# Windowed attention with sinks, then a squared-ReLU MLP, on one core: batch 0's last third loaded before w_out, its second 256 tokens masked by VectorE, scores of the first 256 tokens first

## The chip, the cores and the metric

One core of a Trainium2 chip. The time is device microseconds of one execution. The kernel before took 226.03 us (median of 8 runs, 225.04 to 226.9).

## What is computed

For each of 4 batches and 8 heads (768 tokens, head size 64): attention in which token *t* sees the 128 tokens that end with itself, and the first 4 tokens (the sinks). The heads' outputs side by side are the rows `x` of an MLP with a squared ReLU.

```python
scores = scale * np.matmul(q, k.transpose(0, 1, 3, 2))
keep = is_sink | in_window          # pos < 4, or 0 <= t - pos < 128
scores = np.where(keep, scores, -1000000000.0)
a = np.exp(scores - np.max(scores, axis=-1, keepdims=True))
a = a / (np.sum(a, axis=-1, keepdims=True) + 1e-09)
x = np.matmul(a, v)                 # to (B * S, H * D) = (3072, 512)
r = np.maximum(x @ w_in, 0.0)       # w_in 512 x 2048
return (r * r) @ w_out              # w_out 2048 x 512
```

## The kernel before, in words

**Work per batch.** A batch's 768 tokens are three steps `s` of 256; its 8 heads are four pairs `m`. For batches 0 and 1, q and k arrive as f32 in `qr` (line 348), are cast and regrouped into `qs` (helper lines 206, 208, 210 by engine), turned by TensorE into the PSUM tile `pt` (476), and copied into `qkT` by two copies for each `pt`. They are loaded in two groups, the first 512 tokens (group 0) and the last 256 (group 1). For batches 2 and 3 the loads cast (`qn`, 380) and the DMA turns (436).

Then, for each step and pair: scores into `ps` (571), exp on ScalarE into `expm` (590), a mask, and values times `expm` into `po` (634), with the sinks of tokens beyond 256 from a tile `pk` of their own (531, exp 539). Row sums come with `po`: VectorE takes reciprocals (645) and scales into `xn_sb` (646). `px` (671) turns it, a copy puts it in `xT`. Layer 1 is `pm` (694), its ReLU on ScalarE (703), its square on VectorE into `gT` (710); layer 2 is `py` (734), copied to `osb` and stored (750). Below, `b0 s1` is batch 0's step 1.

**Two ways to mask.** In general the mask is a multiplication of `expm` by the tile `mask` (`mask0` for step 0, whose sinks lie inside) on VectorE (599), or a selection on GpSimd (222). In batch 0 with `s < BIASED = 2` there is none: two matmuls of `bias` with the identity (564) put -30000 into `ps` before the scores. The mask tiles are built by GpSimd late (`build_masks`, 252 to 257), from `tri`.

**Order.** Nothing is scheduled on the chip. While the program is built, `Plan.run` (58) takes at each step, among the operations whose predecessors are planned, the one with the earliest planned start, then the lowest key, and puts it on the engine that would end it first. `PE_SLACK`, a DMA's `margin`, the costs in the braces and the keys (`at(...)`, `LO`, `HI`) act on that order alone. Each engine then executes its list in order. PSUM has four tiles, two in the pool `att`, two in `den`; `pm` and `py` take `den` tiles.

**Loads.** SP issues the `qr` loads; GpSimd issues `v` (361, called v0 to v5 for batch 0's six tiles), `w_in` (300, quarters 0 to 3) and `w_out` (307, quarters 0 to 3). `behind` makes an issue wait until another load has landed. Before: SP's group 1 of batch 0 waits for w_out 0; GpSimd issues w_in 0 to 3, w_out 0 and 1, then waits for group 1's second k load, issues w_out 2, v4, v5, w_out 3; SP's loads of batch 1 wait for v5.

```python
    load_w_out(0, None, ())
    load_w_out(1, None, ())
    for m0 in (0, 2):
        for ti in (1, 0):
            load_qk(0, m0, ti, 1, 2, ("w_out", 0) if m0 == 0 and ti == 1 else None, [("w_out", 1)])
    load_w_out(2, ("qk", 0, 2, 1, 1), [("qk", 0, 2, 0, 1)])
    load_v(0, 2, None, ())
    load_w_out(3, None, ())
```

TensorE's list begins with turns and 72 filler matmuls (201) that work on the identity while data is awaited; then all of b0 s0 and s1 up to `px`; then 128 `pm` (four blocks of 16 for each step); then `py` of steps 0 and 1 (64), mixed with step 2 and batch 1.

Of the kernel before, what the change touches and what calls it, by code (L numbers as in the profile page):

```python
# [16 lines left out]
LATENCY = 0.2  # L17
PE_SLACK = 0.334
DMA_START = {"sp": 1.2, "act": 1.2, "pool": 1.6}
# [114 lines left out]
def kernel(  # L134
# [11 lines left out]
    nc = tc.nc  # L146
# [11 lines left out]
    NSINK = 4  # L158
# [92 lines left out]

    def build_masks(e):
        for h2 in range(2):
            for i in range(2):
                nc.gpsimd.tensor_copy(out=mask[:, h2, 2 * i:2 * i + 2, :], in_=tri)
                nc.gpsimd.tensor_copy(out=mask0[:, h2, 2 * i:2 * i + 2, :], in_=tri)
            nc.gpsimd.memset(mask0[0:NSINK, h2, 1:3, :], 1.0)

# [10 lines left out]
    c_ident = op(-9, {"pool": 0.3}, build_ident)  # L269
    c_tri = op(-0.15, {"pool": 0.6}, build_triangles)  # L270
    c_bias = op(-8, {"pool": 1.3}, build_bias)
    c_sinks = op(-7, {"pool": 0.5}, build_head_rows)


# [93 lines left out]
    def load_natural(b, s, older_values):  # L368

        begun = [ops["layer1", b - 2, 0, 0], w_out_op[3]]  # L370
        for ti in (1, 0):
            if s == 0:
                qn_slot[b, ti] = Slot("qr", NT)
            for i in range(2):
                t = 2 * s + i

                def run(e, t=t, ti=ti):
                    if t == 0:
                        qn_t[b, ti] = work["qr"].tile([128, NT, DM], BF16, name="qn", tag="qr")
                    return [nc.gpsimd.dma_start(  # L380
                        out=qn_t[b, ti][:, t, :].rearrange("p (h d) -> p h d", d=D),
                        in_=(q, k)[ti][b, :, 128 * t:128 * t + 128, :].rearrange("h p d -> p h d"))]
                o = dma_op("pool", ("qk", b, ti, t), run, 64 * 0.032,
                           None,
                           [qn_slot[b, ti]] if t == 0 else ())
                o.after += begun
                o.margin = 1.661
        for t in (2 * s, 2 * s + 1):
            def run(e, t=t):
                return [nc.gpsimd.dma_start(  # L390
                    out=v_sb[b % 2][:, t, :, 0:D],
                    in_=v[b, :, 128 * t:128 * t + 128, :].rearrange("h p d -> p h d"))]
            o = dma_op("pool", ("v", b, t), run, 64 * 0.032)
            o.after += begun + older_values
            o.margin = 1.661

# [5 lines left out]
    def attention(b, key):  # L402
# [16 lines left out]
        def stage(g, f0, f1, side):  # L419
# [9 lines left out]
            if b in NATURAL:  # L429
                for s in range(NS):  # L430
                    for ti in (1, 0):
                        for i in range(2):
                            t = 2 * s + i

                            def turn(e, s=s, ti=ti, i=i, t=t):
                                nc.sync.dma_start_transpose(
                                    out=qkT_sb[:, :, ti, t, :], in_=qn_t[b, ti][:, t, :])
                            ops["turn", b, ti, t] = op(
                                at(0.1 * s), {"sp": 1.25}, turn, dma=0.3, reads=[qn_slot[b, ti]],
                                after=[ops["qk", b, ti, t]] + prev_scores + prev_sinks)  # L440
                            ops["turn", b, ti, t].margin = 5.167
                            copies.append(ops["turn", b, ti, t])
                    ops["cast", b, s] = ops["v", b, 2 * s + 1]
# [101 lines left out]
            for s in range(t0 // 256, last // 256):  # L545
# [3 lines left out]
                for m0 in (0, 2):  # L549
# [26 lines left out]
                    sc = []  # L576
                    for ms in ((m0,), (m0 + 1,)) if b == 0 else ((m0, m0 + 1),):
                        sc.append(op(
# [3 lines left out]
                                   for t in range(max(0, 2 * s - 1), 2 * s + 2)] if b in NATURAL else  # L582
                            [c for m in ms for gg in range(g + 1) for c in ops["copies", b, m, gg]]))
                        ops["scores", b, s, ms[0]] = sc[-1]
                    masked = []
                    o = 0 if s else 128
                    for j, m in enumerate((m0, m0 + 1)):
# [19 lines left out]
                        if biased:  # L607
                            masked.append(ex)
                            continue
                        first = b == 0 and s < 2  # L610
                        masked.append(op(at(fm + 0.03), {"pool": 1.3} if first else
                                         {"pool": 1.3, "dve": 0.7} if s else {"dve": 0.58, "pool": 1.1},
                                         domask, after=[ex] if first else [ex, late["masks"]]))

# [39 lines left out]
                if b in NATURAL or b == 1 and s in TURNED:  # L654
                    for t in (2 * s, 2 * s + 1):
                        def turn_x(e, t=t):
# [3 lines left out]
                                ([o_] if t % 2 else []))  # L660
                        o_.margin = 2.284
                    ops["bridge", b, s] = ops["xT", b, s] = o_
# [113 lines left out]

    NATURAL, TURNED, BIASED = (2, 3), (), 2
    load_sinks("act", 0)
# [7 lines left out]
    for i in range(4):  # L786
        load_w_in(i, None if i == 0 else None)
    load_w_out(0, None, ())
    load_w_out(1, None, ())
    for m0 in (0, 2):  # L790
        for ti in (1, 0):
            load_qk(0, m0, ti, 1, 2, ("w_out", 0) if m0 == 0 and ti == 1 else None, [("w_out", 1)])
    load_w_out(2, ("qk", 0, 2, 1, 1), [("qk", 0, 2, 0, 1)])
    load_v(0, 2, None, ())
    load_w_out(3, None, ())
    for m0 in (0, 2):
        for ti in (1, 0):
            load_qk(1, m0, ti, 0, 2, ("v", 0, 5) if m0 == 0 and ti == 1 else None, [("w_out", 3)])
    for m0 in (0, 2):
# [5 lines left out]

    LO, HI = 0.12, 0.624
    for b in range(B):
        if b == 0:
            at = attention(0, lambda f: f - 1.0)
            at(0, 0.0, 1.0, ("den", "att"))  # L810
            late["masks"] = op(0.006, {"pool": 3.0}, build_masks, after=[c_tri, ops["bridge", 0, 1]])
            at(1, 0.2, 0.725, "att")
        if b == 0:
# [3 lines left out]
        else:  # L817
            for i, fb in enumerate(range(0, NFB, 2)):
                layer1(b, b + 0.34 * i / 8, (fb, fb + 1), 0, 512, (0, 1))
        for i, fb in enumerate(range(0, NFB, 4)):  # L820
            if b == 0:
                layer1(b, 0.2 + 0.226 * i / 4, range(fb, fb + 4), 512, 256, (2,))
            else:
                layer1(b, b + 0.34 + 0.167 * i / 4, range(fb, fb + 4), 512, 256, (2,))
        if b + 1 < B:
# [3 lines left out]
            if b == 0:  # L829
                at = attention(1, lambda f: f)  # L830
                at(0, 0.179, 0.751, ("att", "den"))
                at(1, 0.369, 0.369, ("att", "den"))
            else:
                attention(b + 1, lambda f, b=b: b + LO + (HI - LO) * f)(0, 0.0, 1.0, "att")
        for u in range(NS):
            if b == 0 and u < 2:
                layer2(b, u, lambda i, part, u=u: 0.408 + 0.466 * (4 * part + 2 * u + i) / 24, by_part=True)
            else:
# [37 lines left out]
```

The softmax here doesn't subtract the row's maximum and nothing guards it: scores larger than these inputs give would overflow.

## Time and profile before

| | |
|---|---|
| median of 8 runs | 226.03 us |
| the profiled execution | 225.62 us, of it the span 223.9 us |
| mean granted TensorE clock | 1.000 |
| TensorE (PE) busy | 216.9 us, 97% of the span |
| VectorE (DVE), ScalarE (ACT), GpSimd (POOL) busy | 104.0, 115.9, 65.1 us |
| `py`, line 734 | 384 matmuls, 88.5 us |
| `pm`, line 694 | 576 matmuls, 86.7 us |
| HBM read, written | 27.30 MB, 6.29 MB |
| chain that ended last, by line | pm 38%, py 38%, po 6%, ps 5% |

All times are counted from the first instruction of the span. In a timeline, the first number is the start, the second the length; a bracket tells how long the engine was idle before and what ended that. The chain is the work that ended last, followed back from the end. A matmul's own duration (379 ns for 512 columns) contains its passage through the array; back to back they are issued faster (1.73 us for 8 of them in the chain).

### The profile page before, as it was taken

What the parts mean: (1) busy time and instruction counts of PE and PEld (TensorE: products, weight loads), DVE (VectorE), ACT (ScalarE), POOL (GpSimd) and SP (SyncE); (2) the same over time, 40 slices, a digit from 0 to 9 for tenths busy, and PEclk for the clock granted to TensorE, in tenths of its full rate; (3) what the DMA queues carried; (4) which work ended last, traced back from release to release, by engine and by line L of the source; (5) the groups of instructions that cost most, each with busy time, mean ns of one, the idle gap of its engine ahead of it and who ended that gap; (6) DMA issues with size and microseconds to landing.
All of it is one profiled execution on the core that took longest, in us unless ns stands there. A gap on an engine that the chain in (4) does not pass through costs nothing.

```text
span 223.9 us, 4606 instructions
## 1 busy us (share of the span) xinstructions
PE 216.9 (97%) x1952; PEld 138.0 (62%) x1952; DVE 104.0 (46%) x192; ACT 115.9 (52%) x131; POOL 65.1 (29%) x99
## 2 busy tenths in 40 slices
PE   7899999999999999999999999999999999999993
PEld 7549996467865896555454545598464455874441
DVE  6656356466756764466462536657241024430010
ACT  2695556506893577286727188665351165551010
POOL 7991015046999335996300000000000000000000
PEclk9999999999999999999999999999999999999999
DMA  6999976998999999999999463020221320000222
GB/s 179 258 161 208 214 212 101 225 327 244 129 179 136 141 201 140 106 155 204 145 141 150 139 165 49 0 50 0 47 97 25 117 97 0 0 3 0 94 103 86
DMA packets 84309, 28.13 MB, mean 126 GB/s; under 512 B 70336, under 2 KB 80832, under 8 KB 84288
## 3 DMA queue, kind: packets, MB, share of 16 engines
q0 software_dynamic: 52608, 10.49, 58.9%
q1 hardware_dynamic: 31496, 17.20, 35.4%
q8 instruction: 15, 0.25, 0.5%
q10 hardware_dynamic: 184, 0.14, 0.2%
q14 instruction: 6, 0.05, 0.1%
HBM read 27.30 MB, written 6.29 MB: 150 GB/s over the span
## 4 chain that ended last, share of the span: by engine, by line
PE 91%; DMA 3%; SPq 1%; ACT 1%; DVE 1%; issue 0%; DVEq 0%
PE pm L694 38%; PE py L734 38%; PE po L634 6%; PE ps L571 5%; DMA qr<-in_q_dram 3%; PE pt L476 2%; SPq L348 1%; PE px L671 1%; DVE qkT L208 1%; PE ps L564 1%; PE pk L531 0%; ACT r L703 0%; ACT expm L590 0%; DVE qs L208 0%; ACT qkT L206 0%
## 5 line engine op out<-in xcount | busy, mean ns | idle before, releaser
L734 PE MATMUL py<-w_out_sb,gT 128*128 128x512 bf16 x384 | 88.5, 379 | 0.0
L694 PE MATMUL pm<-xT,w_in_sb 128*128 128x256 bf16 (+1 forms) x576 | 86.7, 308 | 0.4 <-ACT r L703 0.3
L694 PEld LDWEIGHTS <-w_in_sb 128*128 128x128 bf16 x576 | 62.9, 114 | 20.9 <-issue 1.7
L703 ACT ACTIVATE r<-pm 128x1024 bf16<-128x1024 f32 x48 | 49.2, 1026 | 32.6 <-PE pm L694 24.6
L734 PEld LDWEIGHTS <-gT 128*128 128x128 bf16 x384 | 35.4, 98 | 39.2 <-issue 1.7
L710 DVE TENSOR_TENSOR gT<-r 128x1024 bf16<-128x1024 bf16 x48 | 33.5, 698 | 49.9 <-ACT r L703 49.8
L590 ACT ACTIVATE expm<-ps 128x1024 bf16<-128x1024 f32 (+1 forms) x48 | 43.2, 951 | 17.1 <-PE ps L571 17.1
L599 DVE TENSOR_TENSOR expm<-expm,mask 128x1024 bf16<-128x1024 bf16 (+1 forms) x39 | 25.4, 654 | 23.7 <-ACT expm L590 23.2
L206 ACT ACTIVATE osb<-py 128x1024 f32<-128x1024 f32 x9 | 9.2, 1024 | 31.2 <-PE py L734 31.1
L634 PEld LDWEIGHTS <-expm 128*128 128x128 bf16 x352 | 16.5, 97 | 4.1 <-issue 0.6
L634 PE MATMUL po<-v,expm 128*128 128x65 bf16 x352 | 17.5, 193 | 0.0
L646 DVE TENSOR_TENSOR xn_sb<-po,rc 128x512 bf16<-128x512 f32 x24 | 16.6, 691 | 0.8
L571 PE MATMUL ps<-qkT 64*128 64x128 bf16 (+1 forms) x256 | 14.8, 238 | 0.0
L571 PEld LDWEIGHTS <-qkT 64*128 64x128 bf16 x256 | 8.0, 94 | 10.7 <-issue 9.9
L634 PE MATMUL po<-vs,es 128*128 128x65 bf16 x128 | 13.1, 193 | 0.0
L390 POOL DMA_DIRECT2D v<-in_v_dram x12 | 10.7, 904 | 6.1 <-DMA qn<-in_q_dram 6.1
L208 DVE COPY osb<-py 128x1024 f32<-128x1024 f32 (+2 forms) x4 | 3.6, 890 | 19.0 <-PE py L734 15.9
L210 POOL CAST qs<-qr 128x512 bf16<-128x512 f32 x6 | 4.1, 694 | 26.7 <-DMA qr<-in_q_dram 14.9
L634 PEld LDWEIGHTS <-es 128*128 128x128 bf16 x128 | 11.7, 97 | 0.0
L380 POOL DMA_DIRECT2D qn<-in_q_dram x12 | 10.8, 914 | 2.4 <-DMA qn<-in_k_dram 2.3
L208 DVE CAST qs<-qr 128x512 bf16<-128x512 f32 x16 | 8.1, 511 | 6.8 <-DMA qr<-in_k_dram 3.4
L361 POOL DMA_DIRECT2D v<-in_v_dram x12 | 11.1, 942 | 0.6 <-DMA qr<-in_k_dram 0.6
(51 smaller groups left out, 108.1 us busy)
## 6 DMA issues: line engine op xcount, KB each, us to landing
out_dram<-osb SPq DMA_DIRECT2D x11, 512.0 KB, 2.8
v<-in_v_dram POOLq DMA_DIRECT2D x24, 128.0 KB, 6.7
qr<-in_k_dram SPq DMA_DIRECT2D x8, 256.0 KB, 5.2
qr<-in_q_dram SPq DMA_DIRECT2D x8, 256.0 KB, 5.0
w_in_sb<-in_moe_w_in_dram POOLq DMA_DIRECT2D x4, 512.0 KB, 10.5
w_out_sb<-in_moe_w_out_dram POOLq DMA_DIRECT2D x4, 512.0 KB, 11.0
qn<-in_k_dram POOLq DMA_DIRECT2D x12, 128.0 KB, 7.7
qn<-in_q_dram POOLq DMA_DIRECT2D x12, 128.0 KB, 10.5
```

Source lines behind the costliest of these rows:

```text
L208: nc.vector.tensor_copy(out=dst, in_=src)
L361: return [nc.gpsimd.dma_start(out=v_sb[b % 2][:, t, :, 0:D], in_=v[b, :, 128 * t:128 * t + 128, :].rearrange("h p d -> p h d"))]
L380: return [nc.gpsimd.dma_start(out=qn_t[b, ti][:, t, :].rearrange("p (h d) -> p h d", d=D), in_=(q, k)[ti][b, :, 128 * t:128 * t + 128, :]. ...
L571: nc.tensor.matmul(ps[:, h2, o:o + w], lhsT=qkT_sb[r, m, 1, c, :], rhs=qkT_sb[r, m, 0, qb:qb + w // 128, :], start=(i == 0 and not biased) ...
L590: nc.scalar.activation(out=x[:, :, o:512], in_=bank_t["s", b, s, m][:, :, o:512], func=AF.Exp, scale=scale)
L599: nc.vector.tensor_mul(x[:, :, o:512], x[:, :, o:512], mk[:, :, o:512])
L634: nc.tensor.matmul(pv[:, i, h2, :], lhsT=lhsT, rhs=rhs, start=(n_ == 0), stop=(n_ == len(mms) - 1))
L646: nc.vector.tensor_tensor(out=xn_sb[:, 2 * s:2 * s + 2, 128 * m0:128 * m0 + 256].rearrange("p i (j h d) -> p j i h d", j=2, d=D), in0=pv[: ...
L694: nc.tensor.matmul(pm[:, i, :], lhsT=w_in_sb[:, fb // 4, kb, fb % 4:512:4], rhs=xT[:, c0 // 256:(c0 + cw) // 256, kb, :], start=(kb == 0), ...
L703: nc.scalar.activation(out=r, in_=bank_t.pop(tag), func=AF.Relu)
L710: (nc.vector if e == "dve" else nc.gpsimd).tensor_mul(gT_sb[c0 // 512][:, fbs[0]:fbs[0] + n, c0 % 512:c0 % 512 + cw], r, r)
L734: nc.tensor.matmul(pm[:, i, :], lhsT=gT_sb[t // 4][:, fb, 128 * (t % 4):128 * (t % 4) + 128], rhs=w_out_sb[:, fb, :], start=(fb == 0), sto ...
```

## The change

- b0 s1 gets no bias matmuls any more (`BIASED` 2 to 1): it is masked like the other steps, by VectorE here. `mask` is built early and by VectorE, `mask0` by GpSimd before layer 1; `tri` moves ahead of `bias` in GpSimd's list.
- `FIRST`: b0's scores of step 1 are planned behind those of step 0, pairs 2 and 3. `SINGLE`: from step 2 on, batch 0's scores of two pairs are one operation.
- Loads: group 1 of batch 0 waits for w_in 2, then v4 and v5 behind its second k load, and only then all of w_out; batch 1's loads wait for w_out 2. w_in 0 waits for the last k load of group 0.
- Keys, margins, `PE_SLACK`, `LO`, `HI` and the PSUM pools of some stages are others, which changes orders.

```diff
-PE_SLACK = 0.334
+PE_SLACK = 0.319
...
-    def build_masks(e):
+    def build_mask(e):
+        eng = nc.vector if e == "dve" else nc.gpsimd
         for h2 in range(2):
             for i in range(2):
-                nc.gpsimd.tensor_copy(out=mask[:, h2, 2 * i:2 * i + 2, :], in_=tri)
-                nc.gpsimd.tensor_copy(out=mask0[:, h2, 2 * i:2 * i + 2, :], in_=tri)
-            nc.gpsimd.memset(mask0[0:NSINK, h2, 1:3, :], 1.0)
+                eng.tensor_copy(out=mask[:, h2, 2 * i:2 * i + 2, :], in_=tri)
+
+    def build_mask0(e):
+        eng = nc.vector if e == "dve" else nc.gpsimd
+        for h2 in range(2):
+            for i in range(2):
+                eng.tensor_copy(out=mask0[:, h2, 2 * i:2 * i + 2, :], in_=tri)
+            eng.memset(mask0[0:NSINK, h2, 1:3, :], 1.0)
...
-    c_tri = op(-0.15, {"pool": 0.6}, build_triangles)
+    c_tri = op(-8.5, {"pool": 0.6}, build_triangles)
...
+    c_mask = op(-6, {"dve": 0.65, "pool": 1.6}, build_mask, after=[c_tri])
...
-                o.margin = 1.661
+                o.margin = 2.172
...
-                            ops["turn", b, ti, t].margin = 5.167
+                            ops["turn", b, ti, t].margin = 3.561
...
-                    for ms in ((m0,), (m0 + 1,)) if b == 0 else ((m0, m0 + 1),):
+                    for ms in ((m0,), (m0 + 1,)) if b == 0 and s < SINGLE else ((m0, m0 + 1),):
...
-                            [c for m in ms for gg in range(g + 1) for c in ops["copies", b, m, gg]]))
+                            [c for m in ms for gg in range(g + 1) for c in ops["copies", b, m, gg]] +
+                            ([ops["scores", b, 0, x] for x in FIRST[m0]] if b == 0 and s == 1 else [])))
...
-                        first = b == 0 and s < 2
-                        masked.append(op(at(fm + 0.03), {"pool": 1.3} if first else
-                                         {"pool": 1.3, "dve": 0.7} if s else {"dve": 0.58, "pool": 1.1},
-                                         domask, after=[ex] if first else [ex, late["masks"]]))
+                        masked.append(op(at(fm + 0.03), {"pool": 1.3, "dve": 0.7} if s else {"dve": 0.58, "pool": 1.1},
+                                         domask, after=[ex, c_mask if s else late["mask0"]]))
...
-                        o_.margin = 2.284
+                        o_.margin = 2.0
...
-    NATURAL, TURNED, BIASED = (2, 3), (), 2
+    NATURAL, TURNED, BIASED, SINGLE = (2, 3), (), 1, 2
+    FIRST = {0: (2, 3), 2: (2, 3)}
...
-        load_w_in(i, None if i == 0 else None)
+        load_w_in(i, ("qk", 0, 3, 1, 0) if i == 0 else None)
+    for m0 in (0, 2):
+        for ti in (1, 0):
+            load_qk(0, m0, ti, 1, 2, ("w_in", 2) if m0 == 0 and ti == 1 else None, [("w_in", 3)])
+    load_v(0, 2, ("qk", 0, 2, 1, 1), [("qk", 0, 2, 0, 1)])
     load_w_out(0, None, ())
     load_w_out(1, None, ())
-    for m0 in (0, 2):
-        for ti in (1, 0):
-            load_qk(0, m0, ti, 1, 2, ("w_out", 0) if m0 == 0 and ti == 1 else None, [("w_out", 1)])
-    load_w_out(2, ("qk", 0, 2, 1, 1), [("qk", 0, 2, 0, 1)])
-    load_v(0, 2, None, ())
+    load_w_out(2, None, ())
     load_w_out(3, None, ())
     for m0 in (0, 2):
         for ti in (1, 0):
-            load_qk(1, m0, ti, 0, 2, ("v", 0, 5) if m0 == 0 and ti == 1 else None, [("w_out", 3)])
+            load_qk(1, m0, ti, 0, 2, ("w_out", 2) if m0 == 0 and ti == 1 else None, [("w_out", 3)])
...
-    LO, HI = 0.12, 0.624
+    LO, HI = 0.056, 0.645
...
-            late["masks"] = op(0.006, {"pool": 3.0}, build_masks, after=[c_tri, ops["bridge", 0, 1]])
-            at(1, 0.2, 0.725, "att")
+            late["mask0"] = op(-0.01, {"pool": 1.8, "dve": 0.8}, build_mask0, after=[c_tri, ops["bridge", 0, 1]])
+            at(1, 0.765, 1.417, ("att", "den"))
...
-                layer1(b, b + 0.34 * i / 8, (fb, fb + 1), 0, 512, (0, 1))
+                layer1(b, b + 0.343 * i / 8, (fb, fb + 1), 0, 512, (0, 1))
...
-                layer1(b, 0.2 + 0.226 * i / 4, range(fb, fb + 4), 512, 256, (2,))
+                layer1(b, 0.242 + 0.121 * i / 4, range(fb, fb + 4), 512, 256, (2,))
...
-                at(0, 0.179, 0.751, ("att", "den"))
-                at(1, 0.369, 0.369, ("att", "den"))
+                at(0, 0.064, 0.727, "att")
+                at(1, 0.257, 0.2, ("att", "den"))
...
-                layer2(b, u, lambda i, part, u=u: 0.408 + 0.466 * (4 * part + 2 * u + i) / 24, by_part=True)
+                layer2(b, u, lambda i, part, u=u: 0.459 + 0.45 * (4 * part + 2 * u + i) / 24, by_part=True)
```

More of the change, by code (lines that the diff above doesn't have):

```diff
@@ L394, in load_natural @@
             o.after += begun + older_values
-            o.margin = 1.661
+            o.margin = 2.172
     def load_sinks(queue, b):
@@ L818 @@
             for i, fb in enumerate(range(0, NFB, 2)):
-                layer1(b, b + 0.34 * i / 8, (fb, fb + 1), 0, 512, (0, 1))
+                layer1(b, b + 0.343 * i / 8, (fb, fb + 1), 0, 512, (0, 1))
         for i, fb in enumerate(range(0, NFB, 4)):
             if b == 0:
-                layer1(b, 0.2 + 0.226 * i / 4, range(fb, fb + 4), 512, 256, (2,))
+                layer1(b, 0.242 + 0.121 * i / 4, range(fb, fb + 4), 512, 256, (2,))
             else:
-                layer1(b, b + 0.34 + 0.167 * i / 4, range(fb, fb + 4), 512, 256, (2,))
+                layer1(b, b + 0.343 + 0.167 * i / 4, range(fb, fb + 4), 512, 256, (2,))
         if b + 1 < B:
```

## The prediction

> **What bounds the kernel now.** First the page: which engine is full, and when; then the chain that ended last.
>
> ```profile
> PE   7899999999999999999999999999999999999993
> ...
> PEclk9999999999999999999999999999999999999999
> DMA  6999976998999999999999463020221320000222
> ...
> PE 91%; DMA 3%; SPq 1%; ACT 1%; DVE 1%; issue 0%; DVEq 0%
> ```
>
> TensorE is full from the third slice to the last at the full clock, and 91% of the chain is its work: a change counts by the TensorE work it removes and the TensorE waits it makes or ends. The chain in order of time tells where waits are:
>
> ```profile
> 20.36 0.53 PE px L671 x8
> 20.91 14.13 PE pm L694 x128
> 35.04 0.45 PE pt L476 x8
> 35.49 1.73 PE py L734 x8
> ...
> 61.69 1.03 ACT r L703
> ...
> 220.04 0.39 ACT half L206
> ```
>
> To 20.91 us lies the front: loads, then the chain through attention. From there to 220.04 only one wait is seen, 1.03 us for a ReLU. I test this by counting TensorE's list from 35.49 with the chain's rates: 8 py 1.73 us, 16 pm 1.75 (256 columns) or 3.45 (512), 24 po 0.73, 12 po 0.365, 6 or 12 ps 0.33 or 0.55 plus 0.11 for the change back (4 py behind ps take 0.97 instead of 0.86), 8 pt or px 0.45, 4 pk 0.22 or 0.33. That gives 183.65 us and an end at 219.14; measured 220.04. The missing 0.90 is the ReLU wait. So what can still be won lies in the front and in that wait.
>
> **The front.** The timeline shows what ends last there:
>
> ```profile
> 10.31 0.69 DVE L208 CAST qs<-qr 128x512 bf16<-128x512 f32 x1 [0.34 <-DMA qr<-in_q_dram]
> 10.92 1.87 DVE L208 COPY qkT<-pt 128x512 bf16<-128x512 bf16 x3
> 13.32 1.72 ACT L590 ACTIVATE expm<-ps 128x1024 bf16<-128x1024 f32 x2
> 15.29 2.80 ACT L590 ACTIVATE expm<-ps 128x768 bf16<-128x768 f32 x3
> 19.84 2.12 ACT L206 ACTIVATE xT<-px 128x1024 bf16<-128x1024 bf16 x2 [1.74 <-PE px L671]
> ```
>
> After the last q load VectorE and ScalarE copy qkT, ScalarE runs eight exps, and pm waits for all of them, since both steps' values stand ahead of it.
>
> *Removed:* eight bias matmuls of 512 columns, four pairs of 0.54 us in the chain: 2.16 us, in the front. *Moved:* b0 s0 comes first. On ScalarE in the new order, with starts apart 0.67 us for an exp of 768, 0.92 for one of 1024, 0.5 for a qkT copy, 0.38 for the es exp (from these rows): the second copy of a pt waits for the first, on VectorE until 11.6; copy 11.6, exp 12.1, copy 12.8, exps 13.3 and 14.0, es 14.6, three exps of b0 s1 from 15.0, xT copy of s0 at 17.8, done 18.8. TensorE has px ready by 17: norm of the second pairs 15.3 to 16.2, then px 0.45. So pm starts at about **18.9** instead of 20.91. Behind it, 128 pm take 14.0, the po of s1's second pairs 0.73, px of s1 0.45, two pt 0.90, two pairs of scores 0.66, pk 0.22: first py possible at **35.9**. w_in keeps up: quarters land 7.8, 9.6, 11.4 and 13.2 us after issue, at 17.8, 20.3, 22.8 and 25.4, and are first needed at 18.9, 20.7, 23.3 and 25.5.
>
> At no cost, each with its cover:
> - Four mask copies (128x256) on VectorE ahead of the first cast. Not in the trace on this engine; bounds from 0 to GpSimd's 0.40 each. I take 0.27, a VectorE memset of that size, 1.1 in all. The first pt goes from 5.5 to about 6.1; the second pair's k lands only at 6.4, and VectorE idles 1.38 us there. At 0.40 it would still be covered, by the 1.2 us shown below.
> - Four mask multiplications, 4 x 0.70, fall where VectorE idles 2.52 us before 17.49 and 2.50 before 23.91. They lie behind the exps on the path of s1's values, which now have 32 pm (3.5 us) in front of them.
> - GpSimd: tri (0.85) before bias delays bias0 from 3.2 to 4.1, used at 7.9. Four mask copies (1.6) leave, mask0's 2.2 stay in an idle stretch of 14.95 us. w_in 0's added wait ends at 9.5, while GpSimd issues v until 9.97.
> - One exp of batch 1 is masked by a GpSimd multiplication in the midst of its load issues, in place of two selections (2 x 0.64). Bounds 0.55 (VectorE's row) to 1.3; I take 1.1. Queued behind are batch 2's loads; the fourth turn lands 8.9 us after 71.2, at 80.1, and is used at 88.2. Cover 8 us.
> - An output store moves ahead of the last turn of batch 2 on SP; it waits for py near 95, the turn's reader is near 108.
> - Three more fillers (201) stand in waits.
>
> **Where it is given back: w_out.**
>
> ```profile
> 27.86 0.39 SPq L348 DMA_DIRECT2D qr<-in_k_dram  x1
> 34.29 0.53 POOL L307 DMA_DIRECT2D w_out_sb<-in_moe_w_out_dram  x1 [1.12 <-DMA qr<-in_k_dram]
> 34.81 1.97 POOL L361 DMA_DIRECT2D v<-in_v_dram  x2
> 36.76 0.57 POOL L307 DMA_DIRECT2D w_out_sb<-in_moe_w_out_dram  x1
> 41.52 0.37 SPq L348 DMA_DIRECT2D qr<-in_k_dram  x1
> ```
>
> Before, w_out 0 was issued at 12.9 and landed 14.9 later, at 27.8, 7.7 us before py wanted it. Now group 1 is issued when w_in 2 lands, 22.8, that is 5.05 earlier, under the same load (one 512 KB load still in flight, 2.5 us). Its second k load landed at 33.8 and lands at 28.7; GpSimd issued 0.5 after that, now at 29.25: v4 and v5 (1.97), and w_out 0 from 31.2. A v on an empty queue lands 4.3 (issue at 55.17) to 5.2 (issue at 6.22) later; the next 1.0 behind it; w_out behind a v 2.3 later (41.5 to 43.8). With 4.5, since SP's queue is empty too: 29.25 + 4.5 + 1.05 + 2.3 = **37.1**. Bounds: 36.3, if it took only the 5.1 of the w_out issued alone at 34.29; 37.9 with 5.2 and 2.5. TensorE stands from 35.9 to 37.15 with py next in its list; what could fill the gap comes after.
>
> The Trainium skill prices this otherwise: "DMA: Bandwidth & Descriptors", section "Anatomy of one DMA — SWDGE (gpsimd) path", fits 2.0 us plus bytes over 436 thousand per us, 3.2 us for 512 KB. By it, an estimate, w_out 0 would land at 34.4, nobody would wait, and the time would be 224.7 us. The trace's lone w_out took 5.1, so I go by the rows.
>
> **Behind the first py** the new list counts 182.1 us with the same rates: 1.55 less than before, 1.33 done earlier (8 pt, 12 ps with their change, a pk), 0.22 from two fewer changes to scores. New waits, following the lists: batch 1's first q load is issued behind w_out 2, 37.1 + 2 x 2.4 = 41.9 instead of 41.52; its cast could start at 48.6, now 49.0, done 49.45, and pt is wanted at 49.2: 0.3. The pm after the last py needs the den tile that VectorE empties (1.2 us) behind two casts: 0.2. A pk needs the last of a row of copies: 0.25. Sum 0.75; the old 0.90 goes, since layer 1's step 2 now meets other work there.
>
> **The sum.** 37.15 + 182.1 + 0.75 = 220.0, against 220.04. The tail behind it is the same, so the span stays 223.9, and the profiled execution 225.62. That lies 0.41 under the median of the runs; I forecast the median: **226.0 us**. With the bounds (w_out 36.3 to 37.9; waits 0.4 to 1.5) 224.8 to 227.5.
>
> **Rivals.**
> 1. *w_out 0 is in time*, because v4 and v5 do not hold it up or the front takes longer yet waits less later. For it: TensorE's own work would allow 35.9, and the lone w_out took 5.1. With w_out at 36.3 and waits of 0.4: 36.35 + 182.1 + 0.4 = 218.85, 1.2 less: 224.8. At the least 35.9 + 182.1 + 0.2: 224.2. Chance 0.28.
> 2. *Slower: batch 1's q load is what TensorE waits for.* The load is tied to w_out 2, and in slices 8 to 22 the DMA engines are 0.8 to 0.9 busy. From a landing 0.4 us later than I count, each us costs one at pt near 49.2. If w_out lands at 37.9 at 2.5 us spacing and the load takes 1 us more, the cast ends at 51.4 where TensorE comes at 50.0: with the 0.8 of w_out itself 1.8 to 1.9 us later than the forecast, 227.8; half of it gives 226.9. It decides from 0.7 us on. For it: the cast of before waited for that load already (48.58). Against: before, the turn came 0.9 us after the cast. Chance 0.22.
> 3. *The reorder does nothing:* the xT copy stays behind all exps and pm starts at 20.9 as before. Then py comes at 37.9, past w_out: 37.9 + 182.1 + 0.75 = 220.75, 226.75. The order of ScalarE's list speaks against it. Chance 0.08.
>
> **Chances.** Forecast 0.42, with its own range 225.4 to 226.7. 0.3% (0.68 us) is about what a measurement of this kernel tells from no change: faster 0.28, within 0.42, slower 0.30 (rivals 2 and 3). Range 224.7 to 227.3: it leaves out rival 1's last half us and rival 2's upper third.
>
> **What would show it.** Right: first pm near 18.9; no 512-column bias rows; in the chain a DMA piece of w_out of about 1.2 us just before the first py at 37.1; next a short wait at pt near 49. Wrong: first py before 36.5, or no w_out in the chain (rival 1); over 1 us of qr in the chain near 49 (rival 2); first pm after 20 (rival 3); or waits after 60 us, where batches 2 and 3 are loaded, which I cost at nothing.

## The result, and the profile after

The changed kernel takes **228.63 us** (median of 11 runs, 227.55 to 231.59), against 225.83 us for the kernel before (32 runs, 225.04 to 227.55): ratio 1.0131, 95% interval 1.0103 to 1.0158. The forecast was 226.0 us, with a range of 224.7 to 227.3: the kernel is slower than that, and outside the range. Medians here are of all runs; the ratios leave out the few that took over 1.5% longer than the fastest of the same kernel, so a ratio can be lower than that of the two medians.

The first profile of it, which the expectations below speak of, is of an execution of 231.59 us at a lower mean clock (0.993). The profile after that is read here is a second one of the same program, 227.50 us, span 225.8, mean clock 0.999 (run "again" below). First the page:

```profile
PE   7889997999989999999999999999999999999993
...
PEclk9999999999999999999999999999999999999999
DMA  5999889996999999999999755020221320000222
...
PE 69%; DMA 18%; POOL 7%; DVE 2%; issue 1%; ACT 1%; SPq 0%; POOLq 0%; DVEq 0%
```

TensorE's row has holes in slices 7 and 12 that it didn't have before, and the chain that ended last is 69% TensorE, no longer 91%: 18% is DMA. In order of time (start, length, what):

```profile
11.79 11.29 DMA w_in_sb<-in_moe_w_in_dram
...
23.58 4.08 DMA qr<-in_q_dram
...
29.05 1.91 POOL v L368 x2
30.97 6.37 DMA w_out_sb<-in_moe_w_out_dram
...
47.18 6.70 DMA qr<-in_q_dram
...
58.16 1.72 POOL v L368 x2
59.88 7.63 DMA v<-in_v_dram
67.55 0.77 PE po L640 x20
68.32 0.55 PE ps L578 x12
```

Up to 67.55 us the end is set by loads that wait for each other: w_in 2, group 1, v4 and v5, w_out 0, then batch 1's q, k and v. From 67.55 on it is TensorE's list. TensorE's waits behind the front:

```profile
PE py L740 <- DMA w_out_sb<-in_moe_w_out_dram: 1.1, 1, 1.1
PE po L640 <- DMA v<-in_v_dram: 0.8, 1, 0.8
PE pk L538 <- DVE qkT L208: 0.5, 1, 0.5
```

To see where the time is, I count each profile's list of matmuls at the issue rates of the prediction; what an interval lasts beyond that is lost in it (an estimate, in us, sums good to about 0.4):

| profile | list | lost to 30 | 30 to 40 | 40 to 66 | 66 to 74 |
|---|---|---|---|---|---|
| before, 225.62 | 212.0 | 6.1 | 0.2 | 0.5 | 0.2 |
| changed, 227.50 | 210.1 | 7.4 | 1.2 | 0.8 | 1.4 |

The list is 1.9 us shorter, as meant. Against that, and each time more than before, the front loses 1.3, the stretch with w_out 1.0, that with pk 0.3, and that with the v loads of batch 1 1.2. The last is the wait that the prediction doesn't have at all. This profile is of the fastest of its six runs: it is 1.9 us slower than the profile before, where the medians are 2.8 apart. The first profile (231.59) has the same two waits, longer: 1.40 us for w_out and 1.88 for v.

### The profile page after: what moved, and what is told of

It is laid out like the page before. It is cut to its first block, busy times and chain, and to the rows that moved or that the text cites. A ratio compares the mean times of both kernels' runs of the same rounds, so it can differ in the third digit from the quotient of the medians.

```text
span 229.9 us, 4598 instructions
## 1 busy us (share of the span) xinstructions
PE 217.1 (94%) x1947; PEld 138.4 (60%) x1947; DVE 107.5 (47%) x200; ACT 115.7 (50%) x132; POOL 63.8 (28%) x93
## 4 chain that ended last, share of the span: by engine, by line
PE 69%; DMA 19%; POOL 6%; DVE 2%; issue 1%; ACT 1%; SPq 0%; POOLq 0%; DVEq 0%
PE py L740 32%; PE pm L700 28%; PE po L640 5%; DMA w_in_sb<-in_moe_w_in_dram 5%; DMA qr<-in_k_dram 4%; PE ps L578 4%; DMA v<-in_v_dram 4%; POOL v L368 3%; DMA w_out_sb<-in_moe_w_out_dram 3%; DMA qr<-in_q_dram 3%; ACT expm L598 1%; DVE osb L208 1%; DVE qs L208 1%; POOL w_in_sb L307 1%; PE px L677 1%
## 5 line engine op out<-in xcount | busy, mean ns | idle before, releaser
L700 PE MATMUL pm<-xT,w_in_sb 128*128 128x256 bf16 (+1 forms) x576 | 87.6, 309 | 0.0
L716 DVE TENSOR_TENSOR gT<-r 128x1024 bf16<-128x1024 bf16 x48 | 33.0, 689 | 45.3 <-ACT r L709 45.3
L607 DVE TENSOR_TENSOR expm<-expm,mask 128x1024 bf16<-128x1024 bf16 (+1 forms) x43 | 28.1, 657 | 23.8 <-ACT expm L598 23.2
L206 ACT ACTIVATE osb<-py 128x1024 f32<-128x1024 f32 x10 | 10.3, 1026 | 37.5 <-PE py L740 37.5
L640 PE MATMUL po<-v,expm 128*128 128x65 bf16 x352 | 18.9, 195 | 1.9 <-DMA v<-in_v_dram 1.9
L640 PEld LDWEIGHTS <-expm 128*128 128x128 bf16 x352 | 17.4, 98 | 4.6 <-DVE gT L716 0.6
L640 PE MATMUL po<-vs,es 128*128 128x65 bf16 x128 | 13.7, 196 | 0.0
L651 DVE RECIPROCAL rc<-po 128x8 f32<-128x8 f32 x24 | 5.0, 207 | 17.5 <-PE po L640 17.4
L521 POOL TENSOR_TENSOR vs<-vs_in,head_rows 32x130 bf16<-32x130 f32 x12 | 5.1, 426 | 21.6 <-PE po L640 21.0
```

Source lines behind the costliest of these rows:

```text
L607: nc.vector.tensor_mul(x[:, :, o:512], x[:, :, o:512], mk[:, :, o:512])
L640: nc.tensor.matmul(pv[:, i, h2, :], lhsT=lhsT, rhs=rhs, start=(n_ == 0), stop=(n_ == len(mms) - 1))
L700: nc.tensor.matmul(pm[:, i, :], lhsT=w_in_sb[:, fb // 4, kb, fb % 4:512:4], rhs=xT[:, c0 // 256:(c0 + cw) // 256, kb, :], start=(kb == 0), ...
L716: (nc.vector if e == "dve" else nc.gpsimd).tensor_mul(gT_sb[c0 // 512][:, fbs[0]:fbs[0] + n, c0 % 512:c0 % 512 + cw], r, r)
```

## The experiments

**On the changed kernel's own lists.** In these kernels every engine's list is the changed kernel's; only what a DMA (or, in one, GpSimd's mask0) waits for, or the place of a DMA in its queue, is altered on the real instructions, not in the plan. Where an issue waits for the landing of another load, I call that a tie. The edits shown are shortened to what they do.

*again:* the changed kernel, unaltered.

> The changed kernel once more, unaltered, for a profile and a time beside the same runs of the kernel before as the three that follow. Its first profile was of an execution of 231.6 us, 3 us above the median. Theory A (loads): two waits of TensorE for loads make the loss, w_out 0 ahead of the first py (1.4 us in the first profile) and the v tiles of batch 1's last third ahead of the values of batch 1 step 2 (1.9 us of idle plus what the list lost around it). It expects both waits here too, smaller, 1 to 2 us each, and 228 to 229 us. Theory B (order): the list itself is worse, for PSUM tiles and copies, and loads matter little. It expects the same time, with waits for other engines of 2 us or more in sum after 40 us.

229.97 us (227.50 to 232.07, 6 runs), ratio 1.0132 [1.0078, 1.0185]. The two waits are theory A's, 1.14 us for w_out and 0.82 for v; for other engines TensorE waits 0.55 us after 40 us, not the 2 of theory B. The runs differ by more than 3 us among themselves; of the 18 runs of the kernel before beside them, 17 lie between 225.4 and 226.3.

*wout_first:* w_out 0 ahead of v4 and v5, behind the same k load.

```diff
-load_v(0, 2, ("qk", 0, 2, 1, 1)); load_w_out(0)
+load_w_out(0, ("qk", 0, 2, 1, 1)); load_v(0, 2)
```

> The changed kernel with the same lists on all engines but GpSimd's DMA issues: w_out 0 goes ahead of v4 and v5 of batch 0, behind the same k load. Theory A: w_out 0 is then alone in its queue and lands about 5 us after 29.7, at 34.8 instead of 38.7; TensorE no longer waits at the first py, 1.4 us less there; since batch 1's loads stay tied to w_out 2, most of it may be lost again at batch 1's v: between 0 and 1.4 us faster than the changed kernel. Theory B: within 0.3 us of the changed kernel.

227.91 us, ratio 1.0096 [1.0062, 1.0131]. That can't be told from the unaltered kernel. Its profile has no w_out wait, but 1.30 for w_in, and 1.40 for v at po.

*b1_early:* batch 1's first q load waits for v5 of batch 0 in place of w_out 2.

> The changed kernel with the same lists; only SP's first load of batch 1 waits for v5 of batch 0 (landed at 35.9 in the first profile) instead of w_out 2 (43.6). Theory A: batch 1's q, k and, behind them, v come up to 5 us earlier, the wait for v ahead of batch 1's step 2 goes; the q and k loads now share the engines with w_out 1 to 3 and may delay them by 2 to 3 us: net 1 to 3 us faster than the changed kernel, the wait at w_out 0 unchanged. Theory B: within 0.3 us of the changed kernel, or slower by the sharing.

228.59 us, 1.0119 [1.0087, 1.0151]: no gain that can be told. The first loads of batch 1 were issued 7.4 us earlier (34.92, against 42.35), but the last third's k landed only 0.3 us earlier (54.36, against 54.70), v5 landed at 67.87 instead of 67.51, and po waited 0.84 for it.

*v1_free:* batch 1's v loads wait for nothing.

```diff
-load_v(1, 0, ("qk", 1, 2, 1, 1))
+load_v(1, 0, None)
```

> The changed kernel with the same lists; only batch 1's v loads wait for nothing but their place in GpSimd's list, where they waited for the k load of batch 1's last third (56.0 in the first profile, GpSimd idle 2.15 us before them). Theory A: v1 to v5 of batch 1 land about 2 us earlier and the wait ahead of step 2's values shrinks by 1 to 2 us: 0.5 to 2 us faster. Theory B: within 0.3 us of the changed kernel.

226.93 us, 1.0061 [1.0034, 1.0088]: the largest gain from a tie alone. No wait for v is left; the first py comes at 37.11, still behind w_out 0 (landed at 37.06).

*v2_last:* v2 of batch 1 is issued behind v3, v4 and v5.

> The changed kernel's lists on every engine, one DMA moved: batch 1's v2 is issued behind its v3, v4 and v5 (order v0, v1, v3, v4, v5, v2). Theory A (the lost time is the loads': step 2's values stand ahead of step 1's in TensorE's list, so the last v to land is the first wanted): v5 lands one place, about 1.0 us, earlier, the wait at po near 67.5 (0.82 us for v5 in the profile of 227.5 us) goes, v2 lands in the last place and is wanted only near 73: 0.5 to 1.5 us below the unaltered changed kernel, ratio 1.003 to 1.010. Theory B (the order of the v loads is nothing; what counts is how many bytes are in flight): nothing moves, the po waits for v4 or v5 as long as before, ratio 1.011 to 1.014.

229.12 us, 1.0122 [1.0077, 1.0167]: no gain. v5 was now fifth of the six, but landed 13.2 us behind k all the same, and po waited 0.46 and 0.82. The row's gaps lie ahead of its second and third load (landings 61.27, 64.41, 67.00), as in the first profile of the unaltered kernel (61.43, 64.93, 66.94), though the third is another v. That theory A reads the lists rightly is not contradicted, but its remedy failed: something else slows the whole row.

*wout_free:* w_out 0 ahead of v4 and v5 and tied to nothing, and v1_free.

> The changed kernel's lists on every engine; w_out 0 is issued right behind w_in 3, ahead of v4 and v5 of batch 0 and waiting for nothing (as in the kernel before), and batch 1's v loads wait for nothing (as in the run that freed them alone, ratio 1.0061). Theory A (loads): w_out 0 lands before 32, no wait at the first py, which comes near 36.0 instead of 37.1 to 37.4; no wait at po near 67: 1.0 to 1.3 us below the run that freed the v loads alone, 225.4 to 226.0 us, ratio 0.999 to 1.002. Rival (w_out 0 is only paid for elsewhere, since group 1 and w_in then share the engines with it): first py near 36 to 37, but pm waits for w_in longer or a later pt waits for q: 226.5 to 227.5, ratio 1.004 to 1.008.

225.99 us, 1.0003 [0.9981, 1.0025]. With both ties gone, the whole loss is gone. But there is no gain over before either. (w_out 0 landed at 33.95, not before 32: GpSimd's cast of qs at 28 stands ahead of it in the list.) Its profile, at 226.58 one of its slower runs, doesn't show what w_out's place saves: pm began late there, at 20.08, and the first py came at 37.39, as in the unaltered kernel.

*stores_small:* what slows the v loads? The first two output stores are issued at 55.56 and 56.9, where v starts; before at 53.20 and 59.2. This kernel stores only 16 of the 256 rows of each, and leaves the others out of the output.

```diff
-nc.sync.dma_start(out=out[128*g:128*g+256, :]..., in_=o)
+nc.sync.dma_start(out=out[128*g:128*g+16, :], in_=o[0:16, 0, :])   # b == 0 and u < 2
```

> The changed kernel; only the first two output stores (batch 0, steps 0 and 1, 512 KB each) are cut to 16 rows, 32 KB each, so those rows of the output are left out. All lists and waits stay. Seen so far: in profiles of the changed lists the time is the landing of batch 1's v5 plus 160.0 to 160.3 us, and v5 lands 12.0 to 14.0 us after batch 1's last third of k (11.5 in the kernel before). Theory D (two stores, issued at 55.6 and 56.9 now, one at 53.2 and one at 59.2 before, move beside the v loads and each takes some 1.7 us from them): v5 lands 9.5 to 10.8 us after k, po waits for v under 0.3 us, 225.8 to 227.2 us, ratio 1.001 to 1.007, and the runs spread less. Rival E (the v loads are slow by themselves, stores or not): v5 still 12 or more after k, 228 to 230 us, ratio 1.010 to 1.018.

226.99 us (226.14 to 227.89), 1.0030 [1.0009, 1.0051]. v5 landed 10.65 us after k instead of 12.8 to 14.0, and the waits behind the front are, in the view of TensorE's waits:

```profile
PE py L740 <- DMA w_out_sb<-in_moe_w_out_dram: 0.8, 1, 0.8
PE pk L538 <- DVE qkT L208: 0.5, 1, 0.5
```

The row for v is gone. Theory D holds for these lists: the stores delay the v loads. (The runs differ by 1.8 us, but that is no sign of its own: those of b1_early, with whole stores, differ by 1.2.)

*stores_hold:* the same two stores, whole, behind the landing of v5.

> The changed kernel, whole output; the first two stores are issued behind the landing of batch 1's v5 instead of as soon as osb is written. Theory D: the v loads have the engines to themselves as with the small stores, v5 lands 9.5 to 10.8 us after k, po waits under 0.3 us; the stores land near 69 and 72, before the third osb tile is wanted near 74: 225.8 to 227.4 us, ratio 1.001 to 1.008. Rival E: v5 as late as before, 228 to 230. A third way: py waits for a den tile because osb is still being stored, a new wait of 1 us or more near 74 in place of that for v: 227.5 to 229.

229.21 us, 1.0122 [1.0080, 1.0163]. No wait for v (v5 11.1 us after k), but the third way came, in another place than I named. VectorE's row and TensorE's in the timeline (kblk holds the sinks' k, which pk reads):

```profile
78.50 0.34 DVE L520 COPY kblk<-qkT 64x16 bf16<-64x16 bf16 x2 [4.83 <-DMA qkT<-qn]
...
79.62 0.24 PE L645 MATMUL po<-v,expm 128*128 128x65 bf16 x2 [2.01 <-DVE expm L612]
```

The stores now stand ahead of batch 2's turns, VectorE idles 4.83 us for a turn, and TensorE's po waits 2.01 us for VectorE at 79.62. Right behind that wait TensorE's clock was at half for 3.41 us (last section), which adds to the loss in this profile. A transfer that is pushed back meets the next.

*before_v_free:* the kernel before, with v1_free's edit.

> The kernel before, lists unaltered; batch 1's v loads wait for nothing instead of the last third's k load. The same edit took the changed kernel from ratio 1.013 to 1.006. Theory C (that tie costs only where the values come early: in the kernel before v5 lands at 66.14, 0.76 us ahead of the first po that may need it, at 66.90): no gain, ratio 0.998 to 1.001; it may lose if the v loads take from the q loads ahead of the turns near 50 to 55. Rival (the tie holds up both kernels): 0.5 to 1 us faster, ratio 0.995 to 0.998.

225.81 us, 0.9983 [0.9961, 1.0006]: nothing that can be told from no change. v5 lands at 66.11 as it did at 66.14, ahead of the first po24 at 66.90. The same tie is harmless there and costs about 1.6 us in the changed kernel (1.0132 to 1.0061). Without it GpSimd issues batch 1's v from 54.50 in the kernel before, 0.67 us earlier than with it; in the changed one from 52.67, 2.58 earlier.

*best1:* wout_free, and batch 1's q load behind v5 of batch 0.

> The changed kernel's lists; w_out 0 issued right behind w_in 3 and waiting for nothing, batch 1's v loads waiting for nothing (both as in the run at ratio 1.0003), and batch 1's first q load tied to v5 of batch 0 instead of w_out 2, some 4 us earlier. Theory A (every late load removed): the pk wait of 0.9 us near 62 shortens, since the last third's q and k land 1 us earlier, 224.8 to 225.6 us, ratio 0.996 to 0.9995. Rival (pk waits for VectorE's own row of casts and copies, not for the loads): 225.7 to 226.3, ratio 1.000 to 1.003.

226.47 us, 1.0013 [0.9993, 1.0034]. The pk wait fell from 0.89 (in wout_free) to 0.54, but in this profile pm waited 1.0 us for w_in: the rival's size, for another reason.

*mask0_late:* in some profiles pm starts late. VectorE's kblk copies and GpSimd's mask0 copies in the timeline, in the changed kernel (227.50 us):

```profile
13.22 0.54 DVE L515 COPY kblk<-qkT 64x16 bf16<-64x16 bf16 x2 [1.20 <-ACT qkT L206]
13.34 0.73 POOL L262 COPY mask<-tri 128x256 bf16<-128x256 bf16 x2
```

and in wout_free:

```profile
13.35 0.73 POOL L262 COPY mask<-tri 128x256 bf16<-128x256 bf16 x2
13.78 1.37 DVE L529 COPY kblk<-qkT 64x16 bf16<-64x16 bf16 x2 [1.26 <-ACT qkT L206]
```

In the first profile they start ahead of GpSimd and take 0.54 us, in the second behind it and take 1.37. The edit makes GpSimd's first mask0 copy wait for the first xT copy.

> The changed kernel's lists; GpSimd's building of mask0 (four copies and two fills, now at 13.3 to 15.4 us) waits for the first xT copy on ScalarE (done near 18.6). Seen so far: VectorE's two kblk copies take 0.45 to 0.54 us where they start ahead of GpSimd's mask copies (13.0 to 13.4 us) and 1.24 to 1.37 us where they start in their midst (13.8 to 14.2), and TensorE's first pm is at 18.5 to 19.0 in the former and 20.1 to 20.4 in the latter; before, they took 0.35. Theory F (those copies are held by GpSimd's): kblk 0.35 to 0.55, first pm at or before 19.3 whatever the loads do. Because w_out 0 and batch 1's v come later than TensorE anyway, the time changes little: 227.3 to 229 us, ratio 1.007 to 1.013, with fewer runs above 230. Rival G (the kblk copies are long for another reason, the q load behind them): they stay at 1.2 or more in executions with a late load, first pm 20 or later, ratio as unaltered, 1.013.

229.02 us, 1.0153 [1.0122, 1.0183]: no gain, a little above F's ratio, and the runs still differ by 3.4 us. kblk took 0.44 us and the first pm came at 18.48, as F says; the two other runs with this edit, best2 and best3, have 0.40 and 0.35, and pm at 18.58 and 18.65. But most profiles without it look the same, so the three agree with F more than they show it, and this isn't what sets the end while w_out and v come later.

*best2:* wout_free and mask0_late together.

> The changed kernel's lists with three delays taken away together: w_out 0 ahead of v4 and v5 and tied to nothing; batch 1's v loads tied to nothing (these two gave ratio 1.0003, with first pm at 20.08 and first py at 37.39 in the profile); GpSimd's mask0 behind the first xT copy. Theories A, D and F together: first pm near 18.7, first py 36.2 to 36.6 (w_in 3 lands near 25.6 and bounds it), no wait for w_out or v: 224.8 to 225.5 us, ratio 0.996 to 0.9995. Rival (pm waits for w_in as long as the front is earlier): first py 37 or later, 225.8 to 226.3, ratio 1.000 to 1.003.

225.90 us, 1.0002 [0.9985, 1.0019]: the rival's result. TensorE's pm in the timeline:

```profile
18.58 1.94 PE L719 MATMUL pm<-xT,w_in_sb 128*128 128x256 bf16 x16 [0.17 <-DMA w_in_sb<-in_moe_w_in_dram]
21.07 1.94 PE L719 MATMUL pm<-xT,w_in_sb 128*128 128x256 bf16 x16 [0.56 <-DMA w_in_sb<-in_moe_w_in_dram]
...
26.23 3.68 PE L719 MATMUL pm<-xT,w_in_sb 128*128 128x256 bf16 x32 [0.23 <-DMA w_in_sb<-in_moe_w_in_dram]
```

pm starts early, and then follows w_in's landings (18.53, 21.03, 23.57, 26.18): first py at 37.16.

**With parts of the change undone, planned anew.** Here the lists differ too.

*old_loads:* the changed kernel with the load list of before.

> The changed kernel with the load list of the kernel before (w_out 0 and 1, then group 1 behind w_out 0, w_out 2, v4, v5, w_out 3; batch 1 behind v5), all else as changed: the masks, the order of scores, keys and margins. The planner follows: the turns of group 1 stand behind all 128 pm again. Theory A (the change's arithmetic part gains, its load part loses): first pm near 18.7, first py near 34 to 35.5 with w_out 0 long landed, no wait for w_out or v: 224.0 to 225.3 us, ratio 0.992 to 0.998. Rival (the arithmetic part gains nothing because group 1 or batch 1 then ends last, or the new order after the first py has waits of its own): 225.6 to 227, ratio 1.000 to 1.006.

230.00 us, 1.0145 [1.0104, 1.0186]. Theory A is refuted in the form it had here: with w_out landed at 28.35 and the first py at 35.17, as it expected, the kernel is as slow. pm waits 1.0 us for xT (at 98.8) and 0.9 for w_in, po 0.54 for an exp and 1.5 for v.

*new_loads:* the kernel before with the load list of the changed one.

> The kernel before with the load list of the changed kernel and nothing else of the change: group 1 behind w_in 2, v4 and v5, then all of w_out; batch 1 behind w_out 2. Masks by bias matmuls, keys and margins as before. Theory A: first pm stays near 20.9, first py near 37 to 37.5, bounded by w_out 0 or just behind it, and batch 1's loads, which now start behind w_out 2, are late for the values near 66 or the turns near 50: 227 to 229 us, ratio 1.005 to 1.015. Rival (the loads alone cost nothing, since w_out 0 lands at 37.1 to 37.4 and this kernel wants it near 37): 225.5 to 226.5, ratio 0.999 to 1.003.

226.49 us, 1.0036 [1.0016, 1.0056]. Between theory (1.005 to 1.015) and rival (0.999 to 1.003). In its profile, 227.36 us and slower than most of its runs, it waits 0.57 for w_out and 0.90 for v.

*old_keys:* masks, score order and loads as changed; keys, margins and PE_SLACK of before.

> The changed kernel's masks, score order and loads, but keys, LO, HI, margins, pools and PE_SLACK of the kernel before. This tells whether the new keys, which bring batch 1's values of step 2 and two output stores together near 55 to 67 us, are what loses. Theory H (the keys): the two first stores are apart again, v5 lands 11.5 to 12 us after k, po does not wait for v or under 0.4 us; w_out 0 still costs about 1 us: 225.5 to 226.8 us, ratio 0.999 to 1.005. Rival (the loads' order alone makes v late): po waits 0.8 us or more for v, 227.5 or more, ratio above 1.008.

228.49 us, 1.0133 [1.0099, 1.0168]. Theory H falls: the stores are apart (54.5 and 59.9), yet v5 lands 12.7 us after k and po waits 0.79. That is the rival's result.

*best3:* old_keys with best2's three edits.

> The run with the keys of before (masks, score order and loads of the changed kernel), with the three edits of the other run of this call: w_out 0 ahead of v4 and v5 and tied to nothing, batch 1's v loads tied to nothing, mask0 behind the first xT copy. If the front's gain is real and only the loads and keys hide it: first py near 36, no waits for loads, 224.0 to 225.2 us, ratio 0.993 to 0.998. If TensorE is then bound by batch 1's q and k (turns near 50 to 57): 225.5 to 226.3, ratio 0.999 to 1.003.

227.44 us, 1.0066 [1.0040, 1.0092]: no wait for loads after the front, but 0.52 for a ReLU at 63.4; outside both expectations.

*masks_only:* the kernel before with the masks and score order alone. *masks_only_v:* the same with v tied to nothing.

> The kernel before with the arithmetic part of the change alone: batch 0's step 1 masked by VectorE in place of bias matmuls, the scores of step 0 first, mask and mask0 built as changed. Loads, keys, margins and PE_SLACK are those of before. So far each run with the new masks and batch 1's v loads tied to k is slow (ratio 1.012 to 1.015), while the new loads under the old masks gave 1.0036. Theory I (with the new masks TensorE's list is 1.9 us shorter, but the front gives it back to w_in, and TensorE then meets batch 1's v, which land no sooner): first pm 18.5 or 20.1, w_in waits, po waits 0.5 to 1.5 us for v: 226.5 to 229, ratio 1.004 to 1.014. Theory A (the new loads are what loses, the arithmetic gains): 224 to 225.3, ratio 0.993 to 0.998.

> As the other kernel of this call, and batch 1's v loads tied to nothing. Theory I: no wait for v at po; what is left is the front, w_in and the waits of the new order: 225 to 226.5, ratio 0.997 to 1.003, 1 us or more below the other kernel. Rival (v is not what this kernel waits for): within 0.5 us of the other kernel.

228.11 us, 1.0110 [1.0090, 1.0129], and 228.45, 1.0122 [1.0093, 1.0151]. So the masks and the score order alone make the kernel 1.1% slower, with the loads of before. Half of theory I falls: v isn't what this list waits for. In the timeline of masks_only:

```profile
63.33 1.02 PE L740 MATMUL py<-w_out_sb,gT 128*128 128x512 bf16 x3 [0.84 <-ACT r L709]
...
73.14 0.23 PE L640 MATMUL po<-v,expm 128*128 128x65 bf16 x2 [0.35 <-DVE expm L607]
...
74.71 0.51 PE L677 MATMUL px<-ident,xn_sb 128*128 128x128 bf16 x6 [0.37 <-DVE xn_sb L652]
...
75.56 0.35 PE L640 MATMUL po<-v,expm 128*128 128x65 bf16 x6 [0.34 <-DVE expm L607]
```

The front gains 0.8 us net (first py at 34.53, before at 35.33), and ScalarE and VectorE take back 1.9 in these four waits, where the list of before has one of 0.34. That is 0.8 of the 1.8 us by which this profile (227.43) is slower than the one before; the rest lies in shorter waits and isn't accounted for.

## Why the prediction was wrong, step by step

- **First pm at 18.9:** right in most executions. It is at 18.46 to 18.96 in 9 of the 14 profiles with the new masks in which mask0's copies wait for nothing of ScalarE's, and at 20.0 to 20.4 in the other five, all with kblk copies of 1.25 to 1.37 us. That mask0's copies "stay in an idle stretch" of GpSimd was true, but not free: the engine beside it paid.
- **"w_in keeps up":** by 0.1 us in my count, with landings taken from one execution. In these profiles w_in 3 lands between 25.3 and 27.0. Of the 2.0 us at pm, at most 0.9 is left at 30 us on the changed lists.
- **w_out 0 at 37.1:** right in size. Where w_out 0 ends the wait on the changed lists, the first py comes at 36.9 to 37.4 in four profiles, and at 38.1, 38.3 and 38.8 in three others, beyond the bounds of 36.3 to 37.9; I took 1.25 us, and the wait is 0.7 to 1.8. The estimate of 3.2 us that the prediction gives beside its rows was too low: w_out 0 took 6.4 us from issue to landing (30.97 to 37.34).
- **New waits, 0.75 us: the step that failed.** From the first py to the last copy the sum has 182.1 + 0.75 = 182.85 us; the profile after has 184.53 (37.39 to 221.92). So 1.7 of the 1.9 us by which its end is later than forecast lie behind the first py, in waits of 2.4 us by the same count of the list, where I had 0.75. pt near 49 (0.3) did not wait, and pk waits 0.5 to 0.9, not 0.25. What the sum leaves out is batch 1's v: the first po24 (a row of 24 matmuls into po) behind the fourth pm is batch 1's step 2, which needs v3 to v5, the last to land, and the prediction puts no wait there.
- **"The old 0.90 goes":** misread. The chain's 1.03 us is the ReLU's length; TensorE idled 0.34 us for it:

```profile
62.77 1.91 PE L694 MATMUL pm<-xT,w_in_sb 128*128 128x256 bf16 x16 [0.34 <-ACT r L703]
```

So most of the 0.90 lay elsewhere in the list, and there was no reason for it to go.
- **The size of the wait for v:** in the kernel before v5 lands at 66.14 and the first po24 is at 66.90, a room of 0.76 us. In the changed one TensorE wants v5 at 66.73 and gets it at 67.51. The two rows, before and after:

```profile
66.90 0.23 PE L634 MATMUL po<-v,expm 128*128 128x65 bf16 x2
67.55 0.19 PE L640 MATMUL po<-v,expm 128*128 128x65 bf16 x1 [0.82 <-DMA v<-in_v_dram]
```

The first two stores, whose new places the prediction doesn't price, lengthen the row of v loads from 11.5 us after k to 12.8 to 14.0. In four of the profiles on the changed lists (again, wout_first, b1_early, mask0_late) the time is the landing of v5 plus 159.97 to 159.99 us: in those v5 alone sets the end.
- **The sign:** the forecast named "waits after 60 us" as what would make it wrong, but for batches 2 and 3. Rival 2 (226.9 to 227.8) came nearest, though the median lies above it, and for a wrong reason: batch 1's q load isn't the one TensorE stands for, and moving it up gave 1.0119.

Shown by removal, on the changed lists: v's tie (1.0132 to 1.0061), w_out 0's place and tie on top of it (to 1.0003), the stores (1.0132 to 1.0030). Not shown by removal, only read from the profiles: that w_in and VectorE take the rest of the front's gain. Open: why v takes 12.7 us after k in old_keys, where the stores are apart, and 12.3 in masks_only; why masks_only loses as much with no wait for loads; and why the lists with new masks wait for different engines under each set of keys. No version here beats the kernel before measurably.

## What to carry over

Before you price a faster front, look up for each later stage how long its data had been there when it was used: here the next stage had 0.76 us of room, so with its loads landing when they did, no gain ahead of it could have been worth more. When a change moves an operation to another step of a list, name the tile it reads, not the kind of operation. And a transfer that is moved is paid by its neighbours in the queues, even where the engine that issues it is idle.

## What the runs showed of the hardware

- **Two 512 KB stores beside six 128 KB loads.** The row of v loads takes 10.65 us after k with the stores cut to 32 KB and 11.1 with them held back, 12.8 to 14.0 with both whole beside it (five profiles on the changed lists, v in its order and tied to k).
- **VectorE behind GpSimd.** Two copies of 64x16 elements, 0.34 to 0.55 us together in nine profiles, took 1.25 to 1.37 in the five where GpSimd's copies of 128x256 had begun before them. In wout_free the second of the two lasts from 14.12 to 15.15, and a GpSimd copy ends at 15.12; in the profile after it lasts from 13.40 to 13.76, and a GpSimd copy ends at 13.73. The Trainium skill has this ("SBUF — State Buffer", section "Who interferes with whom"): a VectorE copy in a mode that uses both ports shares a port pair with GpSimd, and whoever issues first holds it for its whole instruction while the other waits. No view shows the mode of these copies. The ends agree with that, 0.03 us behind GpSimd's in both; but the long copy lasted through a fill and two copies of GpSimd, not one instruction. Having begun later isn't enough either: in new_loads the two took 0.67 us in the midst of GpSimd's copies. Between wout_free and the profile after, kblk starts 0.56 us apart and pm 1.40.
- **Half clock after short waits.** In the execution of 231.59 us po waited three times for v, 1.88 us in all, and from 70.08 us the clock was at half for 3.41 us. The waits, and the windows' row (start:end, length, then busy time and count of PE, PEld, DVE, ACT and POOL, granted clock, DMA share, GB/s):

```profile
68.11 0.19 PE L640 MATMUL po<-v,expm 128*128 128x65 bf16 x1 [0.39 <-DMA v<-in_v_dram]
68.98 0.19 PE L640 MATMUL po<-v,expm 128*128 128x65 bf16 x1 [0.68 <-DMA v<-in_v_dram]
70.05 0.21 PE L640 MATMUL po<-v,expm 128*128 128x65 bf16 x1 [0.81 <-DMA v<-in_v_dram]
```

```profile
70.00:74.00 4.00, 3.96 (x38) 2.43 (x38) 2.33 (x5) 1.94 (x2) 3.59 (x5) 0.57 2.95 149
```

One other profile shows it amid TensorE's work: stores_hold, behind the single wait of 2.01 us shown above, from 79.74 for 3.41 us. "TensorE: Matmul & The Clock Gate", section "HAM oscillation — how this bites in real kernels", in the Trainium skill warns of idle gaps of over about 3.4 us; here no gap was over 2.01, so these two measurements are below it. A single wait of 1.85 us (v2_last, at 38.30) did not bring it. In the 3.41 us ahead of the half clock TensorE was busy 1.52 and 1.40 us; but old_loads has a stretch as long with 1.37 us, and stayed at the full clock. So neither the longest wait nor the busy share alone decides it here, and what does is open. It can be part of why the runs differ so much: of the 20 listed runs of the changed kernel six have a mean clock of 0.989 to 0.993, of 98 of the kernel before none is below 0.996.
